# Loading one weight on GpSimd's queue in two halves, with a newly sought step list, in a fused state-space and linear-attention kernel

## The chip, the cores and the metric

The kernel runs on one core of a Trainium2 chip. Its metric is the device time of one execution in microseconds (us). A core has TensorE (PE in the profile; its weight loads are PEld), VectorE (DVE), ScalarE (ACT), GpSimd (POOL) and SyncE (SP). Transfers are issued by SP, ACT or GpSimd, each from a queue of its own, and are carried out by 16 DMA engines that the queues share.

## The reference, cut to what matters

One input x (2048 rows of 512 columns, bf16) goes through two branches, and a gate mixes them:

```python
g = sigmoid((x * gate_w).sum(-1, keepdims=True))
# branch a: a diagonal complex state-space layer
dt = exp(log_dt);  Lam_bar = exp(dt * Lam)
Bu = x @ (((Lam_bar - 1) / Lam)[:, None] * Bmat).T
h[t] = Lam_bar * h[t-1] + Bu[t]            # 2048 steps, 512 complex states
a = 2 * real(h @ Cmat.T) + x * Dskip
# branch b: linear attention, 32 heads of 16, learned softmax features
q, k, v = split(x @ wqkv)
phi(u) = concat(softmax(u @ w_phi), softmax(-u @ w_phi))
kv = phi(k).T @ v;  z = phi(k).sum(rows)
b = ((phi(q) @ kv) / (phi(q) @ z + 1e-6)) @ wo
out = g * a + (1 - g) * b
```

## The kernel before, in words

x is cut into 16 tiles of 128 rows. Each is loaded by a transposing DMA on SP into `xT` (`x_load`, line 236 of the profile; eight at the start, the rest as steps `l8` to `l15`). Everything is written as small generators, the *steps*, each of which gives up control after a matmul group, an eviction from PSUM or a vector operation:

- `W0` to `W3` transpose K's weight (`wk_nat`, also named `C2r`; tile `ptw`, line 281), `f0` to `f3` fold w_phi into it (`pf`, line 440) and leave `Wk2`. `B` builds the block-diagonal w_phi that `f` uses, from `Wc` and a mask made from the identity matrix.
- `k0` to `k15` multiply a tile with `Wk2` (`pk`, line 484, four matmuls of 512 columns). `q0` to `q15` do the same for Q.
- `u` and `v` multiply a tile with V's weight (`pv`, line 497): `u` takes columns 0 to 255 of `Wv`, `v` columns 256 to 511 and one more, column 512 of the same tile `Wvg`, which holds the gate's weight and is written by step `gw`. Four matmuls each. Evictions go to `vx`, and for `v` one column to `gl`.
- `V`, `U`, `P`, `P2`, `P3`, `P4`, `M` and `D` compute the state-space parameters: `V` transposes the small vectors (`vec_n`, line 317) that GpSimd's queue loads, DVE and ACT compute exponentials, sines and cosines, GpSimd works out the complex coefficients (`M`, up to the copies into `dgB`), DVE spreads them (`D`, lines 430 to 432). `V2` transposes the vectors for the skip term and the gate.
- `x`, `n`, `e` and `s` compute the softmax features of a group of key tiles (maximum, minimum, exponentials on ACT, sums and a product on DVE); `a0` to `a4` accumulate keys times values (`kvacc`, line 599). `X`, `N`, `E`, `S` do it for queries.
- `g`, `z`, `Z`, `h` are the state-space scan in matrix form; `y`, `o`, `t` make the outputs: `o` the attention part, normalised into `on` and transposed to `oT`, mostly by DMA on SP; `t` the last matmuls with `Wo`, the gate and the store.

The order of everything on PE, DVE, ACT and SP is written out by hand in `ORDER`, a list of 911 tokens; each token advances its step by one piece. `@b` gives PSUM banks, `:D` puts an eviction on DVE in place of ACT, `:A` puts a store on ACT's queue in place of SP's, and `F:n` issues n matmuls on a constant (`spin`, line 849). Each engine takes its pieces in the order of this list and waits where an input isn't there. GpSimd's instructions stand in the order of the program text: four constants, the two identity matrices (`ident`, `identf`), the iota, the five small loads (line 258), and later `Dd` and step `M`. `Wv` (512 KB) is loaded on SP, between the first four and the next four tiles of x (line 245).

Of the kernel before, what the change touches and what calls it, by code (L numbers as in the profile page):

```python
# [23 lines left out]
ORDER = """
NI l8 l10 l9 B F:34 W0@4 W0:D W1@5 W1:D NR W2@0 l11 W3@6 W2:D W3 f0@2 l12 l13 l14 R0 f0:D R1 R3 f1@7 f1 l15 R2 R4 Q1
Q0 f2@4 f2:D C4 f3@1 f3 V@5 R5 V U P P P2 P2 P2 P2 P2 P4 P4 P4 P i3 i1 P2 U k0@7 k0 i0 Q2 k2@4 k1@6 k1 V2@2 V2 gw k2
i0 i3 P3 P3 i3 i1 i3:D x0 x0 k3@1 i3 n0 u0@3 u0 x0 v2@2 n0 i1 v3@7 i2 x0 u3@0 v3 u1@5 v2 u3 u1:D k4@3 k3 v4@2 u5@1 k4
k6@4 i2 v4 i2 u5 u4@2 i0 i0:D U u6@7 C3 n0 i2:D v0@0 n0 Q3 i1:D x0 x1 n0 i2 k5@3 U k7@5 v1@1 i1 i0 L u6:D e0 x1 v7@6
k6 k5 C5 k7 n1 n1 u2@3 e0 v5@7 v1 v5 n1 u2 v7 x1 x1 v0 v8@5 u4 n1 x1 n1 n2 k9@4 k9 x2 C0 e1 s0 k8@7 k8 x2 s0 u7@0
k10@6 u8@4 v6@1 k10 M u7 x2 s0 x2 s0 s0 s0 n2 D C6 e1 s1 C2 k11@7 C7 s0 k12@2 k11 k12 k13@3 k14@6 s1 n2 k13 s1 s1 v6  # L30
k14 g40@0 a0@71 g40 n2 s1 a0 x2 u8 n2 n3 x3 s1 s1 g20@3 g20 n3 x3 g60@0 g60 v8 g00@6 g00 g10@3 n3 g10 e2 e2 k15@4 k15
g10 e2 C1 g30@2 a1 J0 x3 x3 a1 n3 g01@0 g01 J2 J3 x3 g30 n3 g30 u11@3 u11 e2 g50@5 g50 g70@3 g50 n4 s2 n4 g41@4 e3 J1
e3 s2 s2 g70 g70 s2 g62@0 g02@2 g62 x4 s2 g11@0 s2 g02 g70 g21@5 g11 g41 g70 e3 e3 n4 g22@4 g61@6 g61 w0@2 w0 x4 g21
s2 g11 g70:D a2 a2 g51@3 a2 g31@2 a2 x4 w3@0 z0 g22 w2@5 w2 z0 n4 g31 g42@4 z0 g31 z0 z0 w3 w1@6 w1 g51 g51 x4 s3 z0
s3 z0 R7 z0 g42 s3 z0 z0 s3 s3 R6 s3 Z0@2 x4 n4 g71@0 Z0 g71 g71 s3 e4 g12@3 g12 g12 q3@4 q3 g71 g71 g71 h10@2 q1@5 q1
h10 c2:D q2@4 q2 e4 h50@3 u10@0 J2 z1 z1 q0@5 q0 e4 h50 h60@4 z1 z1 a3 u10 g32@3 g32 g32 g52@2 z1 z1 h60 xA z1 z1 e4
g52 g52 c3 xA v9@4 z1 c5:D v12@5 v9 c4 z1 Z1@6 s4 J3 g72@2 g72 v12 g03@0 g72 g72 J1 Z1 h51@5 c5 g72 g72 s4 nA s4 v11@4
u14@3 v11 u12@6 v10@2 nA J0 u14 h51 v13@4 s4 s4 v10 g03 v13 v14@3 c5 h11@5 u9@2 z2 g23@0 z2 xA u12 u9 g13@4 a3 s4 g13
z2 z2 z2 z2 v14 h11 z2 z2 c2:D c4 xA z2 z2 v15@6 nA g23 c4 c1 Z2@0 Z2 a3 h61@5 a3 g13 c0 c2 c6 v15 g33@2 c6 nA g43@0
g43 xA nA g33 g33 h61 u15@4 h52@0 h52 h12@3 h12 h20@6 u15 eA u13@2 g53@4 g53 eA eA g53 h22@3 s4 c6 u13 h22 g63@5 g63  # L40
c0 g73@0 h62@4 h62 h21@2 a4 eA h21 g73 g73 a4 a4 q10@3 h20 g73 sA a4 Y h32@5 h32 h31@2 g73 sA g73 z3 z3 sA q4@4 q4 h32
G h31 h30@5 q9@6 q6@4 h31 q8@0 z3 z3 z3 z3 Y Y z3 z3 h30 h42@2 q14@7 q6 c3 q8 Y q9 sA z3 z3 sA sA q10 h30 h41@1 h41
q13@0 c0 c3 sA Z3@4 q14 Z3 q11@6 q11 c1 q13 h40@3 q15@5 sA h13@7 h13 h53@4 O c7 h33@7 q15 q7@6 q5@1 sA h23@0 h33 q5
h42 c1 y6@2 h33 h53 h63@1 h43@4 h40 y2@7 h02@3 h02 sA sA c7:D h23 h01@5 h01 c7 sA y2 h63 G y6 q7 h43 h00@0 h01 h00
h03@4 h03 h02 h00 y6 END X1 o0@3 o0 o0@6 o0 h03 y5@5 o2@1 o2 o2@0 o2 o2 o0 o1@6 o1 y5 N1 y3@3 o1@4 y0@0 y0 X1 N1 X1 N1
X1 N1 q12@6 X1 N1 E1 o3@1 y0 E1 y3 y3 E1 E1 X2 o2 y2 o2 o1 o3 G t2 X2 G o0 o0 q12 X2 N2 X2 N2 o3@1 o3 X2 S1 y8@6 y5 S1
o3 S1 N2 t0 S1 o3 o1 o3 o1 o1 S1 N2 y9@4 y9 y1@1 y1 y8 y8 S1 S1 t2 t0 N2 E2 S1 S1 t3 E2 E2 S1 S1 E2 X3 t3 N3 X3 S1 X3
N3 X3 N3 t2:A y1 t1 t1 y4@7 o4@3 X3 y9 o4 o4@0 o4 o4 S2 S2 y13@1 o4 o4 o5@0 S2 S2 o5 o5@3 N3 o5 o5 o5 o5 S2 S2 y13 y13
o6@0 o6:D o6@3 o6 y4 o6 o6 o6 y7@3 S2 y4 S2 S2 S2 y7 y7 N3 o7@0 o7 t4 t4:D t5 E3 E3 o7@0 o7:D t5:D t6 t6:D S2 S2 E3 o7
o7 o7 y11@7 y11 E3 S3 o8@2 o8 o8@5 o8 o8 o8 y10@0 o9@2 o9 y10 S3 o8 o9@5 o9 S3 S3 S3 S3 y12@2 y12 o9 o11@5 y12 y10 o11  # L50
y11 o9 o9 S3 S3 o10@5 o10 t7 S3 o11@5 t7:D o11 o11 o11 t8 o10@5 o11 o10 o10 o10 S3 S3@3 t8 t9 t1:A t9 o10 S3 S3@5 S3:D
y15@6 o12@4 o12 o12@5 o12:D o12 y15 t3 o14@3 o14:D t6 o14@4 t9:A o14 t8:A y15 t11 t7 t5 t11:D o14 o12 o14 y14@3 o13@4
o15@7 o13:D o13@5 t0 o15 o13:D o13 o13 y14 y14 t11:A o14@4 o12@5 o12 o15@7 t10 o13@5 o13:D o14:D o15 o15 t10 t10:A o15
t12 t13 t4:A t12 t12 o15@7 o15:D t14 t14 t15 t13:D t15:D t13 t15:A t14
"""
# [17 lines left out]
def kernel(  # L73
# [161 lines left out]
    def x_load(ti):  # L235
        nc.sync.dma_start_transpose(out=xT[:, :, ti * P:(ti + 1) * P], in_=x_res[ti // 2, ti % 2])
# [8 lines left out]
    nc.sync.dma_start(out=Wv, in_=B_wqkv[:, 2 * D:3 * D].rearrange("(k p) n -> p k n", p=P))
# [10 lines left out]
    for t_, srcs in ((vec_n, (A_Lambda_im, A_Lambda_re, A_log_dt)), (vec_m, (A_Dskip, gate_w))):  # L256
        for n, src in enumerate(srcs):
            nc.gpsimd.dma_start(out=t_[4 * n:4 * n + 4, :], in_=src.rearrange("(j p) -> j p", p=P))
# [626 lines left out]
```

## Time and profile before

| | us |
|---|---|
| median of 3 runs (lowest to highest) | 154.43 (153.4 to 154.91) |
| the profiled execution | 153.57 |
| its span, first to last instruction | 151.6 |
| PE busy | 145.9 (96%) |
| DVE busy | 133.6 (88%) |
| ACT busy | 128.9 (85%) |
| POOL busy | 14.1 (9%) |

The span is what the trace shows; the execution took some 2 us more around it. "Busy" counts an instruction from start to modelled end, so PE can look busy while it waits less than a matmul's latency. In rows of the timeline and of the chain the first number is the start and the second the length, both in us. A row with `x4` merges four instructions that follow each other.

### The profile page before, as it was taken

The page shows a single profiled execution, that of the slowest core. Times are in us where ns is not written, and L with a number is a line of the kernel's source. Part 1 is how long each engine was busy: PE and PEld are TensorE (multiplying, and loading weights), DVE is VectorE, ACT ScalarE, POOL GpSimd, SP SyncE. Part 2 cuts the span into 40 slices and gives each one's busy share as a digit, 9 for nine tenths or more (in the row PEclk, how much of TensorE's full clock was granted, in tenths as well). Part 3 has the DMA queues.
Part 4 walks back from the last instruction along what each step waited for, and adds up shares of the span by engine and source line. Part 5 has one row for each costly group of instructions (what it writes and reads, how often), then busy time and mean ns, then how long its engine had stood idle before and what let it go on. Part 6 is the DMA issues. An engine that isn't in the chain of part 4 may idle for free.

```text
span 151.6 us, 3470 instructions
## 1 busy us (share of the span) xinstructions
PE 145.9 (96%) x1268; PEld 100.3 (66%) x1268; DVE 133.6 (88%) x322; ACT 128.9 (85%) x310; POOL 14.1 (9%) x47
## 2 busy tenths in 40 slices
PE   7999999999999999999999999999999999989990
PEld 7847665688889975888888455555545554655640
DVE  3889989999999999999999989999999878764651
ACT  3488999989999899999999999999698859666750
POOL 8236960000000000000000000000000000000000
PEclk9999999999999999999999999999999999999999
DMA  4776999475354797910000003913059558859833
GB/s 109 174 210 89 222 176 156 93 95 113 89 91 102 151 198 159 236 59 4 0 4 0 2 0 70 176 35 69 0 73 228 120 127 186 107 117 163 281 104 104
DMA packets 48737, 17.03 MB, mean 112 GB/s; under 512 B 42064, under 2 KB 48720, under 8 KB 48720
## 3 DMA queue, kind: packets, MB, share of 16 engines
q1 hardware_dynamic: 46864, 15.23, 51.9%
q10 hardware_dynamic: 1696, 1.57, 3.2%
q8 instruction: 10, 0.16, 0.5%
q14 instruction: 7, 0.06, 0.2%
q0 software_dynamic: 160, 0.01, 0.1%
HBM read 2.64 MB, written 2.10 MB: 31 GB/s over the span
## 4 chain that ended last, share of the span: by engine, by line
PE 85%; ACT 7%; DVE 3%; DMA 3%; issue 0%; DVEq 0%
PE pgq L619 18%; PE py L754 17%; PE pq L484 9%; PE py L802 9%; PE pv L497 6%; PE pk L484 5%; PE ph L705 4%; DMA oT<-on 3%; PE kvacc L599 3%; PE spin L849 3%; PE pn L773 2%; PE pgq L624 2%; PE py L759 2%; PE pgq L626 2%; ACT Xq L124 2%; ACT vx L124 1%
## 5 line engine op out<-in xcount | busy, mean ns | idle before, releaser
L619 PE MATMUL pgq<-xT,BT 128*128 128x256 bf16 x256 | 31.5, 272 | 0.0
L619 PEld LDWEIGHTS <-BT 128*128 128x128 bf16 x256 | 24.5, 98 | 3.2
L143 ACT ACTIVATE EEk<-EEk 128x1024 bf16<-128x1024 bf16 x20 | 21.1, 1094 | 0.3 <-DVE EEk L540 0.3
L484 PEld LDWEIGHTS <-xT 128*128 128x128 bf16 x128 | 12.2, 97 | 11.1 <-DMA xT<-in_A_x_dram 0.3
L497 PE MATMUL pv<-Wv,xT 128*128 128x256 bf16 (+1 forms) x128 | 16.6, 272 | 0.4 <-ACT Xq L124 0.3
L124 ACT CAST uv<-pgq 128x512 bf16<-128x512 f32 x28 | 16.3, 612 | 0.6 <-PE pgq L619 0.5
L802 PE MATMUL py<-Wo,oT 128*128 128x512 bf16 x64 | 15.9, 379 | 0.5 <-DMA oT<-on 0.5
L484 PE MATMUL pq<-Wq,xT 128*128 128x512 bf16 x64 | 15.8, 378 | 0.0
L484 PE MATMUL pk<-Wk,xT 128*128 128x512 bf16 x64 | 15.3, 379 | 0.0
L497 PEld LDWEIGHTS <-xT 128*128 128x128 bf16 x128 | 12.4, 97 | 3.7 <-issue 0.8
L143 ACT ACTIVATE ld<-pn 128x16 f32<-128x16 f32 x32 | 6.2, 197 | 6.9 <-PE pn L773 5.5
L143 ACT ACTIVATE EEq<-EEq 128x1024 bf16<-128x1024 bf16 x12 | 11.9, 1069 | 0.0
L124 ACT CAST vx<-pv 128x256 bf16<-128x256 f32 x30 | 11.5, 419 | 0.0
L124 ACT CAST nu<-pn 128x256 bf16<-128x256 f32 x26 | 9.7, 384 | 0.0
L561 DVE TENSOR_TENSOR EEk<-EEk,rck 128x4096 bf16<-128x4096 bf16 (+1 forms) x5 | 9.3, 1857 | 0.0
L608 ACT ACTIVATE phT<-X,dgB 128x512 bf16<-128x512 bf16 x12 | 9.3, 788 | 0.0
L773 PEld LDWEIGHTS <-phT 128*128 128x128 bf16 x128 | 6.7, 97 | 3.9 <-DMA phT<-EEk 0.3
L124 ACT CAST Xq<-pq 128x512 bf16<-128x512 f32 x16 | 9.1, 597 | 0.0
L802 PEld LDWEIGHTS <-oT 128*128 128x128 bf16 x64 | 5.5, 97 | 5.2 <-DMA oT<-on 0.8
L124 ACT CAST Xq<-pk 128x512 bf16<-128x512 f32 x16 | 8.9, 619 | 0.0
L781 DVE TENSOR_TENSOR on<-nu,rd 128x512 bf16<-128x512 bf16 x16 | 6.6, 418 | 1.9 <-ACT rd L143 1.7
L524 DVE TENSOR_TENSOR smk<-smk 128x512 bf16<-128x512 bf16 (+4 forms) x18 | 8.1, 449 | 0.1
(189 smaller groups left out, 324.9 us busy)
## 6 DMA issues: line engine op xcount, KB each, us to landing
X<-HM SPq DMA_DIRECT2D x8, 256.0 KB, 4.0
out_dram<-ot ACTq DMA_DIRECT2D x8, 128.0 KB, 2.1
...
C2r<-in_B_wqkv_dram ACTq DMA_DIRECT2D x2, 256.0 KB, 3.5
Wv<-in_B_wqkv_dram SPq DMA_DIRECT2D x1, 512.0 KB, 4.0
Bn<-in_A_B_im_dram SPq DMA_DIRECT2D x1, 512.0 KB, 5.9
Bn<-in_A_B_re_dram SPq DMA_DIRECT2D x1, 512.0 KB, 5.4
Wo<-in_B_wo_dram SPq DMA_DIRECT2D x1, 512.0 KB, 5.0
```

Of the source, the lines that this page charges most:

```text
L124: nc.scalar.copy(out=out_ap, in_=in_ap)
L143: ins = nc.scalar.activation(**kw)
L484: MM(out=pt[:], lhsT=xT[:, kt, ti * P:(ti + 1) * P], rhs=W[:, kt, :], start=(kt == 0), stop=(kt == KT - 1))
L497: MM(out=pv[:], lhsT=xT[:, kt, ti * P:(ti + 1) * P], rhs=Wvg[:, kt, c * hd:(c + 1) * hd + c], start=(kt == 0), stop=(kt == KT - 1))
L524: VT(out=dst, in0=cur[:, :, :, 0:n, :], in1=cur[:, :, :, n:2 * n, :], op=op)
L561: VT(out=E5, in0=E5, in1=rc.to_broadcast([P, L, 2 * NB, Dh, 4]), op=ALU.mult)
L608: nc.scalar.mul(out=t_, in_=x_, mul=c_)
L619: MM(out=pg[:, h, :], lhsT=BT[:, kt, 2 * j + h, :], rhs=xT[:, kt, r * NC:(r + 1) * NC], start=(h == 0 and kt == 0), stop=(r % 2 == 0 and k ...
L754: MM(out=py[:], lhsT=hs(r, t, slice(a * P, (a + 1) * P)), rhs=C2B[t], start=(t == 0), stop=False)
L773: MM(out=pn[:, 4 * m:4 * m + 4, :].rearrange("p h e -> p (h e)"), lhsT=ph[:, 4 * hf + m, :], rhs=KVm[:, 4 * hf + m, :], start=(m == 0), st ...
L781: VT(out=on[:].rearrange("p g h (a b) -> p (g h) a b", b=4), in0=nu[:].rearrange("p c h (a b) -> p (c h) a b", b=4), in1=rd[:].unsqueeze(2 ...
L802: MM(out=py[:], lhsT=oT[:, g, :], rhs=Wo[:, g, :], start=False, stop=(g == HG - 1))
```

## The change

V's weight is no longer loaded in one transfer on SP. It is loaded in two transfers of 256 columns each (256 KB) on GpSimd's queue: the first stands in front of everything else that the program gives GpSimd, the second behind the five small loads. The step list is a new one. It holds the same 911 pieces but 38 spins in place of 34; a few evictions and products change engine (among them the first eviction of `u0` to DVE and that of `u1` to ACT), six stores in place of eight go to ACT's queue, banks are given anew, and the order differs. At the start it now reads `u0`, `k0`, `u1`, `V`, `k2`, `u3`, `V2`, `k1`, `k3`, `v2` on PE, where it read `V`, `k0`, `k2`, `k1`, `V2`, `k3`, `u0`, `v2`, `v3`, `u3`, `u1`.

```diff
-NI l8 l10 l9 B F:34 W0@4 W0:D W1@5 W1:D NR W2@0 l11 W3@6 W2:D W3 f0@2 l12 l13 l14 R0 f0:D R1 R3 f1@7 f1 l15 R2 R4 Q1
-Q0 f2@4 f2:D C4 f3@1 f3 V@5 R5 V U P P P2 P2 P2 P2 P2 P4 P4 P4 P i3 i1 P2 U k0@7 k0 i0 Q2 k2@4 k1@6 k1 V2@2 V2 gw k2
-i0 i3 P3 P3 i3 i1 i3:D x0 x0 k3@1 i3 n0 u0@3 u0 x0 v2@2 n0 i1 v3@7 i2 x0 u3@0 v3 u1@5 v2 u3 u1:D k4@3 k3 v4@2 u5@1 k4
...
+B NI l8 l10 F:38 W0@5 W0:D W1@1 W1:D l9 NR l11 l13 W3@2 W3 W2@4 W2:D l12 l14 f0@3 f1@6 f1 f0:D R0 R1 f3@7 f3 l15 f2@4
+f2:D u0@1 u0:D k0@2 u1@4 k0 V@1 V U R2 P P R3 P2 P2 P2 k2@0 u1 P2 U u3@3 P P2 P2 R5 u3 V2@6 V2 k1@2 k1 P4 k3@5 R4 k2
+gw v2@6 v2 P4 P3 P4 U v4@7 v4 Q1 v3@1 i3 P3 i1 i0 k4@6 Q3 x0 i0 i3 i3 i0 n0 i3:D i3 x0 k3 k5@7 u4@3 k4 v6@4 n0 i1 v3
...
+    def wv_load(c):
+        cs = slice(c * (D // 2), (c + 1) * (D // 2))
+        nc.gpsimd.dma_start(out=Wvg[:, :, cs], in_=B_wqkv[:, 2 * D + cs.start:2 * D + cs.stop].rearrange("(k p) n -> p k n", p=P))
+
+    wv_load(0)
     wk_nat = const.tile([P, KT, D], BF16, name="C2r")
...
     for ti in range(4):
         x_load(ti)
-    nc.sync.dma_start(out=Wv, in_=B_wqkv[:, 2 * D:3 * D].rearrange("(k p) n -> p k n", p=P))
     for ti in range(4, 8):
         x_load(ti)
...
             nc.gpsimd.dma_start(out=t_[4 * n:4 * n + 4, :], in_=src.rearrange("(j p) -> j p", p=P))
+    wv_load(1)
     M2 = stg.tile([P, 4], F32, name="M2", bufs=1)
```

More of the change, by code (lines that the diff above doesn't have):

```diff
@@ L24 @@
 ORDER = """
-NI l8 l10 l9 B F:34 W0@4 W0:D W1@5 W1:D NR W2@0 l11 W3@6 W2:D W3 f0@2 l12 l13 l14 R0 f0:D R1 R3 f1@7 f1 l15 R2 R4 Q1
-Q0 f2@4 f2:D C4 f3@1 f3 V@5 R5 V U P P P2 P2 P2 P2 P2 P4 P4 P4 P i3 i1 P2 U k0@7 k0 i0 Q2 k2@4 k1@6 k1 V2@2 V2 gw k2
-i0 i3 P3 P3 i3 i1 i3:D x0 x0 k3@1 i3 n0 u0@3 u0 x0 v2@2 n0 i1 v3@7 i2 x0 u3@0 v3 u1@5 v2 u3 u1:D k4@3 k3 v4@2 u5@1 k4
-k6@4 i2 v4 i2 u5 u4@2 i0 i0:D U u6@7 C3 n0 i2:D v0@0 n0 Q3 i1:D x0 x1 n0 i2 k5@3 U k7@5 v1@1 i1 i0 L u6:D e0 x1 v7@6
-k6 k5 C5 k7 n1 n1 u2@3 e0 v5@7 v1 v5 n1 u2 v7 x1 x1 v0 v8@5 u4 n1 x1 n1 n2 k9@4 k9 x2 C0 e1 s0 k8@7 k8 x2 s0 u7@0
@@ L30 @@
[L30 to L54, printed above, removed]
+B NI l8 l10 F:38 W0@5 W0:D W1@1 W1:D l9 NR l11 l13 W3@2 W3 W2@4 W2:D l12 l14 f0@3 f1@6 f1 f0:D R0 R1 f3@7 f3 l15 f2@4
@@ new lines @@
+f2:D u0@1 u0:D k0@2 u1@4 k0 V@1 V U R2 P P R3 P2 P2 P2 k2@0 u1 P2 U u3@3 P P2 P2 R5 u3 V2@6 V2 k1@2 k1 P4 k3@5 R4 k2
+gw v2@6 v2 P4 P3 P4 U v4@7 v4 Q1 v3@1 i3 P3 i1 i0 k4@6 Q3 x0 i0 i3 i3 i0 n0 i3:D i3 x0 k3 k5@7 u4@3 k4 v6@4 n0 i1 v3
+Q2 i1 k5 n0 v7@2 x0 u6@6 u4 n0 x0 Q0 i2 U i2 u2@5 C7 v6 k6@0 C3 i0:D C0 x0 i2 i2:D k7@7 i2 i1:D C2 n0 i1 i0 L u2 k6 n1
+u5@1 v5@5 C6 k7 v1@0 v8@7 e0 u6:D e0 M u5 x1 k9@3 v7 n1 k10@4 u8@1 x1 k9 v5 n1 C5 k8@2 k10 x1 C4 v1 n1 x1 C1 x1 v0@5
+n1 e1 x2 n2 x2 u7@4 u7 J0 s0 s0 n2 e1 s0 x2 s0 s0 v0 s0 D k11@6 k13@4 J1 k13 k12@3 k12 k14@5 k8 k11 g40@0 g40 s0 a0@43
@@ new lines @@
+s1 a0 u8 k14 v8 g00@2 g00 g60@1 g60 x2 s1 n2 s1 x2 n2 s1 s1 g10@0 g10 g20@7 s1 k15@1 g10 n2 e2 g41@6 x3 s1 n3 g20 x3
+a1 a1 k15 n3 u11@7 g01@1 x3 n3 x3 e2 u11 g30@0 g30 J3 g50@2 e2 e2 n3 g62@7 g61@5 g30 g50 x3 n3 e3 g01 s2 s2 s2 g62 e3
+n4 g50 s2 s2 s2 g41 g70@1 g02@0 g02 w0@7 g70 g70 g22@2 g70 n4 g11@6 g11 g21@0 w0 g70 w1@7 x4 n4 e3 x4 s2 e3 a2 a2 a2
+g70:D a2 g11 g61 g51@1 w3@5 g21 w3 x4 w2@6 w2 w1 g31@0 g31 g31 z0 z0 g42@5 x4 g51 z0 z0 z0 z0 s3 s3 g22 z0 g51 g71@6
+s3 g71 z0 s3 s3 J2 s3 z0 z0 g71 Z0@7 g12@1 n4 g71 g12 g42 x4 q1@0 n4 e4 g12 Z0 h50@7 s3 g71 g71 q1 e4 h50 q3@5 q3
@@ new lines @@
+h10@1 h10 R7 q2@2 q2 h60@7 z1 z1 v9@6 h60 c3 J2 J3 v12@1 q0@0 q0 v12 R6 g32@7 g32 e4 z1 z1 u10@1 z1 z1 g32 c2:D z1 z1
+e4 g52@2 xA a3 z1 z1 Z1@7 u10 g52 g52 nA c5:D s4 v9 Z1 g72@5 g72 J1 c4 g72 g03@1 xA s4 c5 g72 g72 g72 nA v11@2 u14@0
+u14 u12@7 h51@6 v10@5 u12 u9@0 v11 J0 c2:D c4 c2 g03 u9 v13@7 g23@2 v10 s4 z2 a3 s4 g23 v13 xA a3 a3 s4 s4 z2 h51 c5
+c1 h11@5 z2 c4 g13@1 g13 g13 v15@6 v15 z2 z2 z2 nA c0 z2 z2 c6 xA z2 u15@7 u15 h11 z2 xA v14@2 v14 g43@5 g43 c6 Z2@0
+g33@6 g33 g33 nA Z2 h52@1 nA u13@7 u13 h52 h12@5 h12 h61@0 h20@6 eA eA eA h61 h20 h21@7 g53@2 g53 g53 h21 h22@0 s4 h22
@@ new lines @@
+g63@5 g63 O g73@7 h62@2 h62 q4@1 h32@6 h32 eA c3 g73 g73 a4 c0 a4 sA a4 a4 Y sA q4 g73 g73 g73 q6@2 h31@0 q10@5 q10
+q9@1 Y Y z3 Y z3 q8@7 h32 h30@5 sA z3 z3 q9 h42@4 h31 h31 z3 z3 sA z3 sA h30 h30 z3 q14@3 q15@1 z3 z3 q14 Z3@6 h41@0 G
+sA q6 q13@3 c0 Z3 h41 sA sA q15 q7@5 q11@2 h42 h33@1 c1 c3 c1 sA q13 h53@0 h33 h53 q8 q11 h33 h13@4 c6 sA sA c7 h40@3
+h13 h40 c7 c7 q7 q5@6 q5 y2@7 h23@4 h63@1 h23 h02@2 h43@0 G y2 y2 h03@4 y6@3 h02 h03 h63 h01@5 h01 h43 h00@6 sA END
+o0@0 h02 h03 h00 h00 X1 y6 N1 h01 X1 o0 o0@4 o0 N1 y5@1 o2@6 o1@5 o2 o2@2 o2 o1 X1 N1 o2 y5 y5 o3@0 X1 N1 y0@6 y0 y0
@@ new lines @@
+q12@5 X1 N1 o2 o1@4 o2 X2 o0 o0 X2 N2 X2 E1 E1 E1 o0 E1 o3 o1 y3@2 t2 y6 t0 X2 o3@0 y1@4 o3 N2 X2 y3 y1 o3 o1 G S1 N2
+y8@0 S1 G t2 y3 y9@7 S1 N2 S1 y9 o3 o1 y8 S1 S1 y1 S1 y9 o3 o1 N2 S1 q12 X3 S1 S1 S1 E2 y8 X3 t3 X3 t1 N3 X3 X3 E2 E2
+E2 S2 t0 S1 y4@6 S2 o4@5 t3 t1 o4:D o4@2 o4 S2 y13@4 o4 o4 N3 o5@2 o5 o5@5 y13 y13 o5 o5 S2 S2 N3 o5 S2 o6@2 o6:D o6@5
+o4 y4 o6 N3 o6 o6 S2 S2 o5 o6 S2 S2 S2 S2 y4 o7@5 y7@2 o7 o7@5 o7 o7 N3 o7 o7 t3:A y7 y7 y11@5 t4 t4:D t5 E3 t5:D E3
+E3 E3 t6 t6:D o8@6 o8 o8@1 o8 o8 S3 y11 o8 o8 y10@3 o9@1 o9 o9@6 o9 o9 S3 S3 S3 S3 S3 o9 o9 y10 t2:A y12@1 y12 o11@6
@@ L55 @@
+y11 y12 y10 S3 o11 S3 o10@6 o10 t7 t7:D S3 o11@6 o11 o11 o11 o11 t8 t8 o10@6 S3 S3@2 S3:D o10:D o10 o10 t9 t9 y15@0
+S3@6 S3:D o12@7 o14@2 y15 o12 o12@7 o10 o12 t1 o14:D o14@6 o12 o14:D t11 y14@7 t11 t11 o12 o13@2 o13:D y15 o13@6 o13:D
+o14 o14 o13 o13 o12@5 y14 t0 o12 t5 t10 t8 o15@6 y14 o13@2 o15 o15@5 o15 t12 o13:D o15 o14@6 o15 t10 t12 t4 t13 t10:A
+o15@2 t7 t12:A t9 o14:D t14 t14 o15:D t15 t6:A t13:D t15:D t15:A t13 t14
 """
```

## The prediction

> **What bounds the kernel now.** I read the head of the page first, for whether one engine fills the span.
>
> ```profile
> span 151.6 us, 3470 instructions
> ...
> PE 145.9 (96%) x1268; PEld 100.3 (66%) x1268; DVE 133.6 (88%) x322; ACT 128.9 (85%) x310; POOL 14.1 (9%) x47
> ```
>
> PE is busy for 145.9 of 151.6 us. So the second view is the chain of waits, which says where the end is not set by PE. Columns: start, length, what.
>
> ```profile
> 1.12 3.81 PE spin L849 x34
> 4.92 0.95 PE ptw L281 x16
> 5.90 0.59 ACT Xq L124
> 6.48 1.13 ACT Wk L124 x2
> ...
> 20.27 1.48 PE pv L497 x12
> 21.75 1.73 PE pk L484 x8
> 23.47 0.45 PE pv L497 x4
> ...
> 129.85 4.07 DMA oT<-on
> ```
>
> The reader is to see three stretches. Up to 4.92 us PE spins on a constant while the first weights come in. From 5.87 (4.92 + 0.95) to 20.27 the chain is not on PE at all: it runs over ACT and DVE. From 20.27 on it is PE, with one piece of another kind, the wait for a transposed oT at 129.85. Full pace can be read from the same rows: four pk matmuls take 1.73 / 2 = 0.86 us and four pv matmuls 0.45 us (0.11 each).
>
> The view of waits for PE gives what the profile itself calls idle, beside the first 1.1 us:
>
> ```profile
> PE py L802 <- DMA oT<-on: 0.5, 1, 0.5
> PE pv L497 <- ACT Xq L124: 0.3, 1, 0.3
> ```
>
> Ends of matmuls are modelled, so waits shorter than a matmul's latency hide inside "busy". I get them from counts. The first two rows are the stretch 4.92 to 20.27, for the k and q line and for the v line (the latter counts one matmul that only begins before it ends); the third is all engines from 30 to 120 us, in the order PE, PEld, DVE, ACT, POOL.
>
> ```profile
> 4.92:20.27 15.35, 7.75 (x32) 2.96 (x32) 1.00 0.82 160
> 4.92:20.27 15.35, 6.08 (x49) 4.75 (x49) 1.00 0.82 160
> 30.00:120.00 90.00, 90.00 (x829) 65.70 (x826) 88.20 (x196) 85.36 (x192) 0.00 (x0) 1.00 0.45 86
> ```
>
> At full pace 32 k matmuls are 32 x 0.86 / 4 = 6.9 us and 48 v matmuls 5.4 us. With ptw 0.95 and the 16 pf matmuls at ptw's pace (another 0.95) that is 14.2 of 15.35 us: about **1.2 us of waits** in this stretch. From 30 to 120 us PE has none, but DVE has only 1.8 us and ACT 4.6 us to spare out of 90. So all that a better order can win is 1.2 us early, 0.5 us at the oT wait, and a little in the tail.
>
> **The change part by part.** *Spins.* 38 instead of 34. The row gives 3.81 / 34 = 0.112 us for one, so four more cost 0.45 us. But the ptw matmuls right behind have the same 128 columns and run at 0.95 / 16 = 0.059 us, so the pace doubled by the end of the spins. The four additional spins come after that point: 4 x 0.059 = 0.24 us. I take +0.24, ends 0.24 and 0.45. (The Trainium skill, "TensorE: Matmul & The Clock Gate", Part 1 on the clock gate, says that the first 3.4 us or so of activity run at half rate, and that this is a budget of time and not of matmuls. The pace here doubles after 3.8 us of spinning, which agrees; by that rule the sum has 0.24, by the spin row alone 0.45.)
>
> *The first half of V's weight, first on GpSimd's queue.* The rows of GpSimd (POOL) in the timeline:
>
> ```profile
> 1.23 0.29 POOL masks.py:199 TENSOR_SCALAR_AFFINE_SELECT ident<-ident 128x128 bf16<-128x128 bf16 x1
> ...
> 1.91 0.78 POOL L258 DMA_DIRECT2D vec_n<-in_A_Lambda_im_dram  x1
> ...
> 4.24 0.52 POOL L258 DMA_DIRECT2D vec_m<-in_gate_w_dram  x1
> ```
>
> No load of this size on POOL is in the trace. Its five loads of 1 KB occupy it from 1.91 to 4.76 us, 0.52 to 0.78 each. The page has their packets (160 in all) and, for the queues of other engines, the time to landing (last column):
>
> ```profile
> q0 software_dynamic: 160, 0.01, 0.1%
> ...
> C2r<-in_B_wqkv_dram ACTq DMA_DIRECT2D x2, 256.0 KB, 3.5
> Wv<-in_B_wqkv_dram SPq DMA_DIRECT2D x1, 512.0 KB, 4.0
> ```
>
> Lower bound 0.52 us on POOL. Upper bound: five small loads are 160 packets, 32 each; half of Wv is 512 runs of 512 bytes, 16 times as many, and if POOL's time went with packets that were 16 x 0.52 = 8.3 us. I take 0.78, the nearest row of POOL itself. Behind it wait ident and identf, the iota and the five small loads, all 0.78 later: ident is ready at 1.52 + 0.78 = 2.3 us, and the transposes that read it start at 4.92 + 0.24 = 5.2 us. Nothing is late, with 2.9 us to spare. (The Trainium skill, "DMA: Bandwidth & Descriptors", Anatomy of one DMA, says of this path that many descriptors can be emitted before their number costs anything; no load here is large enough to show it. It speaks for 0.78.)
>
> *DMA engines.* This half now moves beside C2r, which W0 to W3 transpose. In the rows 256 KB more makes a landing 0.5 us later (3.5 to 4.0). The ptw piece of the chain runs without a gap, so C2r's second half was there when its turn came, by 4.92 + 0.95 / 2 = 5.4 us. With the company that is 5.9 at the latest, and it is now asked for at 5.2 + 0.95 / 2 = 5.7. I take 0, ends 0 and 0.5.
>
> *SP's queue and early v work.* The timeline around the old load:
>
> ```profile
> 5.71 1.28 PE L440 MATMUL pf<-BD,Xq 128*128 128x128 bf16 x16
> ...
> 6.57 0.58 SPq L245 DMA_DIRECT2D Wv<-in_B_wqkv_dram  x1
> ...
> 7.11 2.77 PE L484 MATMUL pk<-Wk,xT 128*128 128x512 bf16 x12
> 7.20 5.12 SPq L236 DMA_TRANSPOSE xT<-in_A_x_dram  x4
> ```
>
> SP is free 0.6 us earlier for x tile 4 and everything behind it; PE shows no wait worth naming on those, so this is worth 0. The 16 pf matmuls end their stream at 5.71 + 0.95 = 6.7, the first pk comes at 7.11: 0.45 us in which PE waits for the evictions of Wk. The new list puts u0 there, 4 x 0.11 = 0.44 us of work that is done anyway. That I count whole, **-0.44**. Of the other 0.75 us early I take half, **-0.37** (ends 0 and 0.75), because three u steps are issued before k1 and k3 and so ACT's evictions start sooner. For the oT wait I take half of 0.5, **-0.25**: the new list reshuffles the end, and nothing in it tells whether the wait stays.
>
> *Second half.* POOL comes to it 0.78 later than the end of the small loads, at 5.5 us; issued and landed in 0.78 + 3.5 it is there at 9.8. The first reader is v2. Ahead of it the new list has u0, k0, u1, V, k2, u3, V2, k1, k3 from about 6.9 us on: 3 x 0.45 + 4 x 0.86 = 4.8 us, so 11.7. Spare: 1.9 us. Cost 0.
>
> *Parameter chain.* V, which starts it, moves behind u0, k0 and u1: later by 0.24 + 0.45 + 0.86 + 0.45, about **1.9 us**. What hangs on it:
>
> ```profile
> 19.66 1.86 POOL L423 COPY dgB<-dl 64x48 f32<-64x48 f32 x4
> ...
> 24.33 0.53 DVE L430 CAST phT<-dgB 128x160 bf16<-128x160 f32 x2
> ...
> 28.36 1.22 DVE L561 TENSOR_TENSOR EEk<-EEk,rck 128x2048 bf16<-128x2048 bf16 x1
> ...
> 29.84 0.67 PE L599 MATMUL kvacc<-vx,EEk 128*128 128x68 bf16 x16
> ```
>
> GpSimd's coefficients end at 21.52 and DVE reads them at 24.33: 2.8 us cover 1.9. The feature chain has less: DVE ends the product for the first key group at 29.58 and a0 begins at 29.84. This goes into the rivals. In the other direction, DVE has less to do before that point: eight of its steps in front of g40 in the old list (n2, s1, x2 and others) stand behind it in the new one.
>
> *The list as a whole.* In front of a2, some 45 us into PE's work, the two lists hold the same steps but for three ACT evictions and two steps of DVE; what changes engine is a handful (one product of c7 from DVE to ACT, single evictions of u0, u1, o4, o7, o10, o12, o14 and S3). PE, DVE and ACT keep their totals within 0.5 us. For new waits that no row can show I add **+0.3**, the size of the one ACT wait on record.
>
> Sum: +0.24 - 0.44 - 0.37 - 0.25 + 0.3 = -0.52. The profiled execution took 153.57 us, of which the span is 151.6; it would come to 153.05, span 151.1. The median of the three runs, 154.43 (153.4 to 154.91), lies 0.86 above that execution, so the forecast is 154.43 - 0.52, about **153.9 us**. A measurement here can tell about 1%, 1.5 us, from no change.
>
> **Rivals.** *Faster than forecast.* All 1.2 us of early waits and the oT wait go and nothing new comes: +0.24 - 1.2 - 0.5 = -1.46, 153.0; with a shorter tail a little below. For it: PE is full elsewhere, so any wait removed is a gain. Against: it takes everything at once.
>
> *a0 comes late (slower).* If the 1.9 us of the parameter chain pass through the table load and the exponentials to the first key product, that product ends at 31.5 instead of 29.6 and PE, which takes its steps in order, stands at a0 and holds every g step behind it. Decides as soon as the delay exceeds the 0.26 us between the two rows. Price up to 1.9 us: 153.9 + 1.9 = 155.8, and with one more wait like it over 156. For it: the rows are that close. Against: DVE is relieved in front of it.
>
> *The second half comes late (slower).* If POOL needs 3 us for each half, the second lands 4.4 us later, 14.2, and PE stands at v2 for 2.5 us: 156.4; at 8.3 us each ident itself is late and it is over 160. Decides at 1.9 us beyond the two times 0.78. The Trainium skill, "SBUF — State Buffer", in its box on DVE blocking DMAs, says that loads issued on GpSimd wait while DVE holds the port pair that they share. Here the first small load took 0.78 beside DVE's work and the last 0.52, so 0.26 is what this case shows.
>
> *The change doesn't do what it says.* The halves interleave in memory, and if u0 waited for both it would start at 9.8 instead of 6.9: +2.9, 156.8. Against: pk starts at 7.11, before x tiles 4 to 7 are even issued at 7.20, although they interleave in xT in the same way.
>
> **How the numbers follow.** Forecast 0.50, own range 152.9 to 155.3. Faster rival 0.18, 0.16 of it beyond 1% (below 152.9). a0 late 0.19, 0.12 of it beyond 1% (above 156.0). Second half late 0.11, halves tied 0.02. That gives faster 0.16, same 0.50 + 0.02 + 0.07 = 0.59, slower 0.25. The range 152.4 to 156.4 leaves out about a third of the faster case and most of the last two, under 2 in 10; it takes in the ends of the spins, of C2r and of the early waits.
>
> **What would show it.** Right: ptw starts near 5.2 us, pv right behind pf near 7, no DVE or ACT piece of any length in the chain before 20 us replaced by DMA, POOL's first load under 1 us. Wrong: POOL's load of several us with ident behind it; a wait of PE at kvacc near 30 us or at pv for Wv near 12; or waits for evictions between 30 and 120 us, where now there are none.

## The result, and the profile after

The changed kernel takes 154.75 us (median of 20 runs, 153.8 to 155.8), the kernel before in the same comparison 153.79 us (20 runs, 152.82 to 154.91). The ratio is **1.0054, 95% interval 1.003 to 1.0077**: some 0.83 us slower, between 0.46 and 1.18 us, where 0.52 us faster was forecast. (The two medians lie 0.96 us apart; the ratio takes in all 40 runs and is used from here on.) It is within the 1% that the prediction called no change, and inside its range.

The head of the page after, and the chain of waits (start, length, what):

```profile
span 152.8 us, 3459 instructions
...
PE 145.9 (95%) x1257; PEld 101.2 (66%) x1272; DVE 134.1 (88%) x322; ACT 129.1 (84%) x310; POOL 16.7 (11%) x49
```

```profile
1.11 4.24 PE spin L854 x38
5.35 1.18 PE ptw L286 x16
6.53 1.07 PE pf L445 x16
7.60 0.44 PE pv L502 x4
...
15.09 0.96 ACT Xq L124 x2
...
18.78 1.28 ACT L135
...
20.50 1.58 PE pv L502 x12
...
30.46 0.51 PE kvacc L604 x16
...
130.89 4.20 DMA oT<-on
```

PE's busy time is the same 145.9 us, so by this view the longer span is time in which PE waits. The view is rough: it counts 1257 matmuls to 1272 weight loads, so 15 matmuls have no record. The pv matmuls stand right behind pf (7.60), as the new list has them. But around 15 to 20 us the chain still runs over ACT, to the load of its table (L135), and from there to the unbroken PE stretch. The same piece before, from the chain of that kernel:

```profile
16.91 1.28 ACT L135
```

It starts 1.87 us later (18.78), the PE stretch 0.23 later (20.50 in place of 20.27), and the wait for oT at 130.89 is still there.

GpSimd in the timeline after (start, length, instruction, and in brackets the idle time before it):

```profile
1.32 1.01 POOL L171 DMA_DIRECT2D Wv<-in_B_wqkv_dram  x1 [0.82 <-POOLq L874]
...
2.79 0.29 POOL masks.py:199 TENSOR_SCALAR_AFFINE_SELECT ident<-ident 128x128 bf16<-128x128 bf16 x1
...
3.47 0.56 POOL L262 DMA_DIRECT2D vec_n<-in_A_Lambda_im_dram  x1
...
6.01 0.81 POOL L171 DMA_DIRECT2D Wv<-in_B_wqkv_dram  x1
```

The early half takes 1.01 us and everything behind it is 1.56 us later (the first small load at 3.47, before at 1.91): the load begins at 1.32, where GpSimd's first work behind the constants began at 0.80 before. The queue's row on the page shows how many packets the two halves were:

```profile
q0 software_dynamic: 320, 0.53, 1.4%
```

That is 160 more than before, 80 for each half and not the 512 of the prediction's upper bound.

**One reading carries most of what follows.** Three points of an execution can be set against each other: the first product of the state-space tables (`pgq`, PE), the start of the first query exponentials (`EEq`, ACT, directly behind VectorE's product), and the end. Before, then after, from the timelines of PE and ACT:

```profile
28.96 1.04 PE L619 MATMUL pgq<-xT,BT 128*128 128x256 bf16 x8
102.06 3.96 ACT L143 ACTIVATE EEq<-EEq 128x1024 bf16<-128x1024 bf16 x4
```

```profile
29.43 1.04 PE L624 MATMUL pgq<-xT,BT 128*128 128x256 bf16 x8
102.89 4.03 ACT L143 ACTIVATE EEq<-EEq 128x1024 bf16<-128x1024 bf16 x4
```

From pgq to the exponentials it is 73.10 us before and 73.46 after. The same two rows in the traces of the experiments below give 73.06 to 73.11 in all seven other traces of the old order in which nothing in that stretch was altered, and 73.40 to 73.46 in the five of the new order (e1, e5, e8 and e14 with other loads, spins or steps at the start, and e16 with one step of PE moved). So between 29 and 102 us an execution hardly varies, and **the new order is 0.36 us slower there**, whatever is done with the loads. What varies is the start and the end:

| | pf's end | to pgq | to the exponentials | to the end of the span |
|---|---|---|---|---|
| before | 6.99 | 21.97 | 73.10 | 49.5 |
| after | 7.60 | 21.83 | 73.46 | 49.9 |
| difference | +0.61 | -0.14 | +0.36 | +0.4 |

The first and the last of these four are in good part chance, as the next section shows: over the experiments, pf's end lies between 6.7 and 7.8 us (e14 aside, where pf itself waits), and the last stretch, where nothing in it was altered, between 49.1 and 50.5.

### The profile page after: what moved, and what is told of

The parts are those of the page before. It is cut to its first block, busy times and chain, and to the rows that moved or that the text cites. A ratio compares the mean times of both kernels' runs of the same rounds, so it can differ in the third digit from the quotient of the medians.

```text
span 152.8 us, 3459 instructions
## 1 busy us (share of the span) xinstructions
PE 145.9 (95%) x1257; PEld 101.2 (66%) x1272; DVE 134.1 (88%) x322; ACT 129.1 (84%) x310; POOL 16.7 (11%) x49
## 4 chain that ended last, share of the span: by engine, by line
PE 87%; ACT 5%; DMA 3%; DVE 2%; issue 2%
PE pgq L624 18%; PE py L759 17%; PE py L807 8%; PE pq L489 7%; PE pv L502 7%; PE pk L489 7%; PE ph L710 4%; PE spin L854 3%; DMA oT<-on 3%; PE kvacc L604 3%; PE pn L778 2%; PE pgq L629 2%; PE py L764 2%; PE pgq L631 2%; PE pf L445 1%
## 5 line engine op out<-in xcount | busy, mean ns | idle before, releaser
L807 PE MATMUL py<-Wo,oT 128*128 128x512 bf16 x62 | 15.4, 379 | 0.7 <-DMA oT<-on 0.6
L489 PE MATMUL pq<-Wq,xT 128*128 128x512 bf16 x60 | 14.9, 379 | 0.2
L143 ACT ACTIVATE ld<-pn 128x16 f32<-128x16 f32 x32 | 6.7, 212 | 7.3 <-PE pn L778 7.1
L124 ACT CAST nu<-pn 128x256 bf16<-128x256 f32 x25 | 9.2, 404 | 0.0
L811 ACT ACTIVATE ot<-py,G 128x512 bf16<-128x512 f32 x10 | 6.6, 685 | 2.1 <-PE py L807 1.9
```

Source lines behind the costliest of these rows:

```text
L124: nc.scalar.copy(out=out_ap, in_=in_ap)
L143: ins = nc.scalar.activation(**kw)
L489: MM(out=pt[:], lhsT=xT[:, kt, ti * P:(ti + 1) * P], rhs=W[:, kt, :], start=(kt == 0), stop=(kt == KT - 1))
L807: MM(out=py[:], lhsT=oT[:, g, :], rhs=Wo[:, g, :], start=False, stop=(g == HG - 1))
L811: nc.scalar.mul(out=ot[:], in_=py[:], mul=G[:, ti:ti + 1])
```

## The experiments

### The spins

e1 is the changed kernel with 34 spins, e2 the kernel before with 38, e15 the kernel before with 50.

```diff
-B NI l8 l10 F:38 W0@5 ...
+B NI l8 l10 F:34 W0@5 ...
```

> The changed kernel with 34 spins in place of 38, nothing else. Theory: the four spins run at the slow pace (0.107 us each, as the trace after shows up to 5.14 us) and PE does nothing else instead, so the first weight transpose starts at 4.72 in place of 5.14 us and the span is 0.43 us shorter, about 152.4; ratio to before about 1.003. Rival: the clock rises after a fixed amount of work, then four spins fewer leave four more transposes at the slow pace and only half, 0.2 us, is won; ratio 1.004. Second rival: the first weight isn't there at 4.72 with V's half beside it, PE waits for C2r and nothing is won; ratio 1.0054.

> The kernel before with 38 spins, nothing else. Theory: 0.43 us longer, ratio 1.003. Rival that the clock rises after a fixed amount of work: 0.2 us, ratio 1.0015.

> The kernel before with 50 spins in place of 34. 16 spins take 0.9 us at PE's faster pace (56 ns each) and 1.7 us at its slower one (107 ns). If a later start of PE is passed on whole to the end: 1.006 to 1.011, and so 0.2 to 0.4 us for the four spins of the change. If it is absorbed by waits behind it (for Wk's copies, for V's weight): under 1.003.

Measured: e1 1.0028 (0.9994 to 1.0061), e2 0.9989 (0.996 to 1.0019), e15 1.0033 (1.0003 to 1.0063). e1's interval holds all three of its expected ratios, and e15 lies between its two. Sixteen spins cost 0.5 us (0.05 to 0.97), so four cost about 0.13, between 0.01 and 0.24, if the cost goes with their number. The predicted 0.24 is the upper end of that, and the spins don't carry the result. (e1 against the changed kernel would say 0.4 us, but the two intervals overlap widely.)

e2's interval, -0.62 to 0.29 us, takes in such a cost. The timeline shows what hides it. Spins and ptw of the kernel before and of e2, and the ptw of e13 (below):

```profile
1.12 3.81 PE L849 MATMUL spin<-fillw 128*128 128x128 bf16 x34 [1.12 <-DVE fillw L162]
4.72 1.14 PE L281 MATMUL ptw<-ident,C2r 128*128 128x128 bf16 x16
```

```profile
1.11 3.71 PE L849 MATMUL spin<-fillw 128*128 128x128 bf16 x38 [1.11 <-DVE fillw L162]
4.66 1.06 PE L281 MATMUL ptw<-ident,C2r 128*128 128x128 bf16 x16
```

```profile
4.72 1.91 PE L286 MATMUL ptw<-ident,C2r 128*128 128x128 bf16 x16
```

38 spins in e2 take less time than 34 before, and the same 16 ptw matmuls take 1.06, 1.14 or 1.91 us. The time at which PE's pace doubles (from 107 to 56 ns from one matmul of 128 columns to the next) isn't fixed: by the starts of single matmuls it is 4.9 us before, 4.2 in e2, 5.9 after, 7.1 in e13. Each us by which it comes later costs 1 - 56/107, about 0.48 us. (The Trainium skill, "TensorE: Matmul & The Clock Gate", Part 1, says that the window by which the clock is raised runs freely and doesn't begin with the kernel. The traces agree with that. It puts the variation at 0.5 us to either side; here it is 4.0 to 7.1 us.) With 0.22 us for four spins at the faster pace and (5.9 - 4.9) x 0.48 for the late doubling, the +0.61 in pf's end is accounted for, and most of it comes from when the pace doubled in that one execution.

### Where V's weight is loaded, with the old order

e3 has the kernel before and its order, with the two loads of the change; e4 in addition has u0 directly behind f3. e6 has the old order with the first half on ACT's queue behind C2r and the second on SP at the old place, which leaves GpSimd's instructions where they were; e7 in addition has u0 behind V. e13 has both halves on GpSimd's queue, but behind the five small loads.

```diff
 # e6
+    wv_load(0, nc.scalar)          # behind the two loads of C2r
...
-    nc.sync.dma_start(out=Wv, in_=B_wqkv[:, 2 * D:3 * D].rearrange("(k p) n -> p k n", p=P))
+    wv_load(1, nc.sync)
 # e13, behind the five small loads on GpSimd's queue
+    wv_load(0)
+    wv_load(1)
```

> V's weight in two halves on GpSimd's queue, with the step list of before (34 spins). Theory that the load itself harms nothing: GpSimd's first load takes 1.0 us, the parameters' loads come 1.5 us later than before, V waits for them until about 8.4 us in place of 6.95, and as V stands ahead of k0 in this list PE stands for that long: span 1 to 1.5 us longer, ratio 1.007 to 1.01. Rival: the small loads land sooner than that or the wait is made up by the shorter wait behind it; ratio 1.000 to 1.003.

> As the run before, and u0 moved up in the old list to directly behind f3, its eviction on VectorE. Theory: u0 fills 0.44 us of the wait for the folded weight or for V; against the run without it 0.4 us shorter. If the wait at V is as long as 1.5 us, the ratio to before stays above 1.004; if there is no wait at V, it falls to 0.997.

> The list of before with the same loads on ScalarE's and SP's queues. Beside the run with the old list and GpSimd's load only the queue differs. Theory that the loss there was the wait of V for its vectors, pushed back by GpSimd's load: V is at 6.95 us again where it was 8.28, the first g at 29.0 where it was 30.0, ratio 0.998 to 1.001. Rival that V's half beside C2r and x on the DMA engines costs: x tiles land later, first g after 29.3, ratio above 1.003.

> As the run before, and u0 moved up in the old list to directly behind V, its eviction on VectorE. Theory: from V on the first g comes 21.5 us later in place of 22.0, as in the run with u0 early and GpSimd's load; with V at 6.95 that is 28.5 us, 0.5 us before the kernel before; ratio 0.997. Rival: k0 is what the chain hangs on, u0 delays it by 0.28 us and nothing is won; ratio 1.000 to 1.002.

> The kernel before, its order and its 34 spins, with V's weight loaded on GpSimd's queue in two halves, both behind the five small loads of the parameter vectors and not ahead of them. Theory A (what costs in the runs with the old order is the early half ahead of the parameter vectors, for which V waits): V starts right behind the last pf matmul as in the kernel before, without a wait for vec_n, and the time is 0.998 to 1.002. Rival (the load on GpSimd's queue, or its traffic beside x's transposes, costs wherever it stands): 1.004 to 1.007.

| | ratio to before (95%) | pvt (vec_n) starts |
|---|---|---|
| e3, both loads as in the change | 1.0063 (1.0029 to 1.0096) | 8.28 |
| e4, u0 behind f3 in addition | 1.0052 (1.0021 to 1.0083) | 8.11 |
| e6, early half on ACT | 1.0046 (1.0018 to 1.0073) | 7.85 |
| e7, u0 behind V in addition | 1.0079 (1.0048 to 1.011) | 7.90 |
| e13, both halves behind the small loads | 1.0014 (0.9983 to 1.0045) | 7.74 |

With the old order, the early half alone costs about as much as the whole change: e3, e4, e6 and e7 are clear of 1, and e13 is not (though its interval still overlaps theirs). Of the expectations, e6's rival came true (the first g at 29.58), e3 lies just under its 1.007 to 1.01, and e7 missed both of its ranges. V's transpose of the parameter vectors, in PE's timeline of e3, e7 and e13:

```profile
8.28 0.16 PE L322 MATMUL pvt<-ident,vec_n 12*128 12x12 bf16 x1 [0.57 <-DMA vec_n<-in_A_log_dt_dram]
```

```profile
7.90 0.16 PE L322 MATMUL pvt<-ident,vec_n 12*128 12x12 bf16 x1 [1.12 <-DMA vec_n<-in_A_log_dt_dram]
```

```profile
7.74 0.18 PE L322 MATMUL pvt<-ident,vec_n 12*128 12x12 bf16 x1
```

In e3 the vectors are asked for 1.56 us later, behind the early half. In e6 and e7 they are asked for when they were before (first at 1.91), but land later, with the early half moving beside them on the DMA engines. The list of transfers has the time from issue to landing in its last column, before and in e7:

```profile
vec_n<-in_A_Lambda_im_dram POOLq DMA_DIRECT2D x1, 1.0 KB, 3.5
```

```profile
vec_n<-in_A_Lambda_im_dram POOLq DMA_DIRECT2D x1, 1.0 KB, 5.0
```

With the loads behind the vectors (e13) PE doesn't wait for them, and the loss is gone or small.

How much of the loss one trace shows depends on when PE's pace doubles in it. In e6, e7 and e8 V starts at 7.85, 7.90 and 7.84, although pf ends at 7.50, 6.79 and 6.74: the vectors set that time, and the wait is 0.35, 1.12 and 1.10 us. So from pf's end to pgq e6, whose pace doubled late (6.1 us), needs only 0.1 us more than before (22.08 in place of 21.97), and e7, whose pace doubled at 4.2, needs 1.1 more (23.08). Against the traces of the old start whose pace doubled by 4.9 us (before, e2, e10 and e12, pgq at 28.81 to 28.96), pgq is 0.6 to 0.8 us later in e6, 0.7 to 0.8 in e4, 0.9 to 1.1 in e7 and 1.05 to 1.2 in e3. The ratios say 0.71, 0.80, 1.22 and 0.97 us. That agrees in size, if most executions of the kernel before double as early as that, which one trace can't show.

What stays open is whether loads on GpSimd's queue delay the doubling itself: it came at 4.7 to 7.1 us (mean 6.1) in the eight traces with a load of V on that queue and at 4.0 to 6.5 (mean 4.8) in the ten others. The 1.3 us between the means would make 0.6 us. But e13 has such loads and no loss, and e6 has a loss and no such load; from one trace of each kernel this can't be told from chance.

### The new order with other starts

e5 has the new order and 38 spins with the loads of e6. e8 is e5 with V and the parameter steps ahead of u0. e14 is e8's order with 34 spins, the early half on GpSimd's queue as in the change, and the three loads of vec_n on ACT's queue.

```diff
 # e8
-f2:D u0@1 u0:D k0@2 u1@4 k0 V@1 V U R2 P P R3 P2 P2 P2 k2@0 ...
+V@5 f2:D V U P P P2 P2 P2 P2 P2 u0@1 P u0:D P2 k0@2 u1@4 k0 R2 R3 k2@0 ...
```

> The changed kernel with its step list, but V's first half loaded on ScalarE's queue behind C2r and the second on SP's at the old place; GpSimd's queue is as before. Theory that the new list sets the start (V, which opens the parameter chain, stands behind u0, k0, u1 and comes at about 9.3 us whoever loads): the first g matmul still comes 22.0 us behind the end of pf, as after; ratio 1.003 to 1.005. Rival that GpSimd's load is what costs (ident and the vectors later): the first g comes 0.5 us earlier, ratio 0.999 to 1.001.

> The new list with V and the small parameter steps up to the sine moved ahead of u0, loads as in the run with the new list and ScalarE's queue. Theory that V's place costs: V at about 7 us, the sine's table load at 8.5 in place of 10.4, and the first g 0.5 us or more earlier relative to the end of pf; ratio 0.997 to 0.999. Rival that from pf on PE and ACT are the bound in the new list and not the parameter chain: the first g stays 22.0 us behind the end of pf.

> The changed kernel with 34 spins, with V and the steps on the parameters moved ahead of the first projection by V's weight (the order of e8), and with the three loads of vec_n on ScalarE's queue right behind Wk's and the pinned table, so that they are not behind the early half. Theory A (late parameters cost): V starts near 7 us without a wait for vec_n, VectorE is idle 0.5 to 1 us less in the first 20 us than in the changed kernel (4.8), and the time is 0.998 to 1.003. Rival (the list as a whole and the traffic of the early half cost, and not the parameters): 1.005 to 1.009 as in e8.

Measured: e5 1.0079 (1.0051 to 1.0108), e8 1.0091 (1.0063 to 1.012), e14 1.0316 (1.0275 to 1.0357). e5 is slower than either of its ranges although its pgq comes 22.16 us behind pf's end, about as its theory has it; why is not known. In e8 V starts at 7.84 in place of 9.34 in the changed kernel, with a wait of 1.1 us for vec_n. The late parameters had been my explanation for the slow middle; it falls: from pgq to the exponentials e8 takes 73.41 us, like every execution of the new order. e14 tells nothing on it, because its edit brought a wait of its own. The chain of e14:

```profile
3.94 4.52 DMA xT<-in_A_x_dram
8.46 0.02 issue
8.49 2.07 DMA vec_n<-in_A_log_dt_dram
```

The third load of vec_n was issued only at 8.49, when a transpose of x on SP's queue had landed, and ACT, which takes its instructions in order, did none of its evictions until then. PE waited 2.44 us for them, and behind that wait its granted clock was lower (columns: window, its length, busy time and instructions, granted clock, DMA share, GB/s):

```profile
10.00:14.00 4.00, 3.48 (x17) 0.60 0.41 91
```

VectorE's busy time in the first 20 us, before, after and in e8 (the same columns):

```profile
0.00:20.00 20.00, 16.18 (x73) 1.00 0.76 158
```

```profile
0.00:20.00 20.00, 15.20 (x72) 1.00 0.85 162
```

```profile
0.00:20.00 20.00, 14.88 (x71) 1.00 0.79 157
```

VectorE is 1.0 us more idle at the start after the change, and 1.3 in e8. Not all of this is the order: in e16, whose pf ends as early as before (6.92), it is busy for 15.79 us, 0.4 less than before. And e8, with the most idle time at the start, is no slower than the others from pgq on (73.41), so this idle time doesn't set the 0.36 us.

### Whose lateness is the 0.36 us

One wait of PE in the middle is found with the new order only. PE and VectorE around 58 us after, and in e16, which has e1's kernel with the projection v9 issued ahead of the product h60:

```diff
-h10@1 h10 R7 q2@2 q2 h60@7 z1 z1 v9@6 h60 ...
+h10@1 h10 R7 q2@2 q2 v9@6 h60@7 z1 z1 h60 ...
```

> The changed kernel with 34 spins and one step moved: the projection v9, which waits for nothing, is issued on PE ahead of h60 in place of behind it, so that it lies in the wait for HM at 58.4 us. Theory D (that wait is the loss of the new order): the wait of 0.46 us goes, from 110 us on the steps stand 0.4 us earlier against the first product of the tables than in the changed kernel, and the time is 0.998 to 1.001. Theory E (VectorE sets it, which ends N1 0.35 us later with this order): the wait goes, but from 110 us on nothing moves by more than 0.1 us, since PE waits for VectorE's results there instead, and the time stays at 1.002 to 1.004.

```profile
56.17 2.28 DVE L566 TENSOR_TENSOR EEk<-EEk,rck 128x4096 bf16<-128x4096 bf16 x1
...
58.37 1.28 DVE L714 TENSOR_TENSOR HM<-ph,uv 128x512 bf16<-128x512 f32 x2
...
59.10 0.38 PE L710 MATMUL ph<-HM,dg 128*128 128x256 bf16 x2 [0.29 <-DVE HM L714]
```

```profile
57.87 1.28 DVE L714 TENSOR_TENSOR HM<-ph,uv 128x512 bf16<-128x512 f32 x2
58.15 0.60 PE L502 MATMUL pv<-Wv,xT 128*128 128x257 bf16 x4
58.60 0.38 PE L710 MATMUL ph<-HM,dg 128*128 128x256 bf16 x2
...
59.20 0.60 PE L502 MATMUL pv<-Wv,xT 128*128 128x257 bf16 x4 [0.22 <-DVE HM L714]
```

After, PE needs HM at once while VectorE is still in a product of 2.28 us. With v9 ahead, the wait at h60 is gone, but the next pv now waits for the second of VectorE's additions, which frees its bank (v12 and h10 share bank 1 in the list). The exponentials start 73.46 us after pgq, as in e1 (73.45): **moving PE's work won nothing: the wait is VectorE's, and it moved along**. The ratio is 1.0027 (1.0 to 1.0053), e1's was 1.0028. That is theory E, but for its "the wait goes": it moved on by one instruction.

What VectorE has to do in that stretch can be counted. Its busy time from pgq to the exponentials, before and after:

```profile
28.96:102.06 73.10, 71.92 (x162) 1.00 0.44 84
```

```profile
29.43:102.89 73.46, 72.60 (x163) 1.00 0.44 82
```

The new order gives VectorE 0.68 us more work there and leaves it 0.86 us idle in place of 1.18: +0.68 - 0.32 = +0.36. It is the same in the other traces (72.60 of 73.45 in e1, 72.58 of 73.41 in e8, but 71.93 of 73.10 in e3, which has the old order). Part of it is work that stood ahead of pgq before, among it one sum `smk` of 128x1024 (0.69 us) and one maximum `mxk` (0.22 us); the rest is a balance of other steps that come into the stretch and leave it. The prediction had seen these steps move behind g40 and had read it as relief ("DVE has less to do before that point"); they came into a stretch that had no room for them.

e11 asks what a late VectorE costs: one sum on VectorE that nothing reads stands ahead of the first X1 product.

```diff
-... y6 END X1 o0@3 ...
+... y6 END DX X1 o0@3 ...
+    def st_DX():
+        VT(out=scr[:], in0=xT[:, 0, 0:1024], in1=xT[:, 1, 0:1024], op=ALU.add)
```

> The kernel before with one VectorE sum of 128x1024 added just ahead of the first X1 product, some 0.6 to 0.7 us of work that nothing reads (estimated from the bf16 products of 128x2048 at 1.22 us). Theory A (a late VectorE at 100 us is passed on to the exponentials, to SP's transposes of 1.2 us each and to PE at 133 us): N1 ends 0.6 later, the time is 1.003 to 1.005. Rival (PE alone bounds, and VectorE's lateness at 100 us is covered): 0.999 to 1.001.

```profile
97.72 0.68 DVE L716 TENSOR_TENSOR scr<-xT 128x1024 bf16<-128x1024 bf16 x1
```

It takes 0.68 us, the exponentials start 0.60 later against pgq (73.70), and the time is 1.0017 (0.9993 to 1.0041) of before: 0.26 us, between -0.1 and 0.6. The middle of that is less than half of the 0.60, but the interval takes in all of it. So how much of the 0.36 us of the new order reaches the end stays open, between nothing and the whole.

e12 tried the other sign: the additions of the steps c on GpSimd in place of VectorE, to relieve it of 8 times 0.42 us.

```diff
-        VT(out=out_ap, in0=ta, in1=tb, op=ALU.add)
+        nc.gpsimd.tensor_tensor(out=out_ap, in0=ta, in1=tb, op=ALU.add)
```

> The kernel before with the additions of the steps c moved from VectorE (8 of about 0.42 us, 3.4 us in all) to GpSimd, which is idle there. Theory A (VectorE full from 20 to 100 us sets the tail): N1 ends 0.5 to 3 us earlier, PE's wait for oT near 133 us (0.6) goes, the time is 0.995 to 0.998. Rival (PE bounds, VectorE only just beside it): 0.999 to 1.001. A third (GpSimd's additions take several times 0.42 us, what reads them waits, or VectorE is slowed beside them): over 1.002.

It gives 1.0183 (1.0139 to 1.0227). One addition takes 1.15 us on GpSimd (0.42 on VectorE), and VectorE's short sums and differences H, 213 to 227 ns before, take up to 1097 ns beside it. The rows of that line give minimum, median and maximum in ns, before and in e12:

```profile
L675 DVE TENSOR_TENSOR H<-mc,ms x16: 213/221/227, 51.4 to 88.4; 64x128 bf16<-64x128 bf16 x16
```

```profile
L675 DVE TENSOR_TENSOR H<-mc,ms x16: 207/221/1097, 51.4 to 91.9; 64x128 bf16<-64x128 bf16 x16
```

All five of VectorE's instructions that began during an addition and read both operands from SBUF were held for most of it: three of H, one minimum (1.38 us in place of 0.42) and one subtraction (2.18 in place of 1.22). The additions `HM`, `Bn` and `Wv`, which read one operand from PSUM, were not (0.67 to 0.69 us, as before). (The Trainium skill, "SBUF — State Buffer", section "SBUF: two separate sides", says that the two engines' shared port pair is locked for a whole instruction and the other engine stands still; the maximum here agrees.) The third case of the expectation came true, and the experiment can't say what a relieved VectorE would be worth.

### Half of each order

e9 has the changed kernel up to step Y and the old order from there, e10 the reverse.

> The changed kernel up to step Y (its two loads on GpSimd's queue, its 38 spins, its order of the first 90 us) with the old kernel's order from there to the end. Theory A (the late start costs: V and its parameters 2.4 us later, VectorE 1 us more idle in its first 20 us and full from there to 100 us): the last N1 product on VectorE still ends near 102.8, the time is 1.004 to 1.006 of the kernel before. Rival B (the newly sought order of the tail costs, which needs the third row block's transposes later beside PE): 0.999 to 1.002. Rival C (the four spins alone): 1.002 to 1.003 here and none in the run with the old start.

> The old kernel up to step Y, with the changed kernel's order from there to the end. Theory A: 0.998 to 1.001, the last N1 product near 102.0 to 102.4. Rival B: 1.003 to 1.006, with PE waiting for oT near 133 us at least as long as in the changed kernel (0.9 us).

Measured: e9 1.0295 (1.0247 to 1.0343), e10 1.0113 (1.0082 to 1.0145). Both are slower than either whole and outside all that was expected. The likely reason, argued from the waits, is that at the seam the steps of one order meet those of the other too early. The first row is of PE's waits in e9, the second of those in e10:

```profile
PE pq L489 <- ACT HM L124: 2.0, 1, 2.0
```

```profile
PE ph L705 <- ACT Xq L124: 1.6, 1, 1.6
```

Behind its wait of 2.0 us PE's granted clock is lower in e9 too, which adds to the loss:

```profile
88.00:92.00 4.00, 4.00 (x16) 0.70 0.00 0
```

So they don't tell the halves apart, and the question was taken up by the three points of the first section instead.

## Why the prediction was wrong, step by step

- **Spins, +0.24.** Right in kind, about 0.13 measured (0.01 to 0.24). The pace was taken to double at a fixed time; it does not (4.0 to 7.1 us).
- **u0 in the gap ahead of pk, -0.44, and half of the other early waits, -0.37.** This is the step that failed. u0 does stand in the gap, yet from pf's end to pgq the changed kernel gains 0.14 us and e1 0.12, not 0.81, with the same steps of PE ahead of pgq in both lists. With the pace doubling at 4.7 us, as early as before, e16 has pgq at 28.93 with 34 spins, the kernel before at 28.96: nothing gained. I had counted work put into a gap of PE as a gain, although the prediction's own chain ran over ACT and VectorE up to 20.27. PE reaches the steps behind that point when ACT has done its evictions, tables and table load, and these got no earlier (18.78 in place of 16.91 for the table load, and 18.28 in e16): by these chains, the waits moved behind the work that was brought forward.
- **The oT wait, -0.25.** Failed. The wait of 0.5 is now 0.6 in two pieces, and over the traces of both orders it is 0.2 to 1.1 or not listed at all. SP issues its transposes there one behind the other, and not at an even pace. SP's queue after:

```profile
129.57 4.89 SPq L800 DMA_TRANSPOSE oT<-on  x3
134.57 1.25 SPq L589 DMA_TRANSPOSE phT<-EEq  x1
```

  One takes 1.25 us, three took 4.89 and not 3.75. Why is not known; before, three took 4.90.
- **New waits, +0.3.** The size was right (0.36 from pgq to the exponentials), its place was not: it is no sum of small waits of PE, but 0.68 us more work for VectorE, which the prediction named as full (1.8 us to spare), whose later steps it read as relief, and which it then left out of the sum. That the size agrees is luck.
- **First half on GpSimd, 0.78.** 1.01 us, and 0.52 more because the first instruction there began later. The upper bound of 8.3 us is excluded; it also took each half for 512 packets, where the queue shows 80. "Nothing is late" held for ident. It missed the small loads behind it: they were weighed against V's late place in the new order, not as transfers beside others on the same DMA engines.
- **DMA engines, 0 to 0.5.** Taken as 0 for C2r, and the contention is there: in e5, where PE comes to ptw early, it waits 0.2 us for C2r. What suffered more is what the term left out, the 1 KB loads, by up to 1.6 us where the half goes on ACT's queue (5.1 from issue to landing in e5, 3.5 before).
- **Rivals.** The second half wasn't late, and the halves aren't tied together: pv runs at 7.44 with the second half issued only at 6.01 (4.4 us to landing, median of the two). a0 isn't late: kvacc stands at 30.46 in the chain, 29.84 before, which is the same 0.6 later as pf's end. Of the signs of being wrong only the last came, a wait of PE between 30 and 120 us (59.10). The result lies between the forecast and that rival, by other causes.

```profile
7.44 0.60 PE L502 MATMUL pv<-Wv,xT 128*128 128x256 bf16 x4
```

Added up, spins 0.13, the start -0.14 to 0, and up to 0.36 for the middle give 0.0 to 0.5 of the 0.83 us measured (0.46 to 1.18). With 34 spins the new order measures 0.4 us (e1 and e16, each between about 0 and 0.9), near the 0.36 of the middle. From the forecast's side, the two early terms (0.7 to 0.8 us not won) and the oT wait (0.25) make up 0.9 to 1.1 of the 1.35 us between -0.52 and +0.83. The early half ahead of the parameter vectors costs by itself with the old order (e3, e4, e6 and e7 against e13); how much of it acts in the changed kernel, where V no longer waits for the vectors, stays open, and so does the rest of the sum.
